# Layer 1's input features in another order, so that the recurrence's output is multiplied straight to its rows

## The chip, the cores and the metric

One core of a Trainium2 chip. The metric is the device time of the whole kernel in microseconds, as a median of runs. TensorE (PE) multiplies, VectorE (DVE) and ScalarE (ACT) do elementwise work and copies, GpSimd (POOL) a little of it, and SyncE (SP) issues nearly all transfers. TensorE writes to PSUM, eight banks of 128 partitions with 512 float32 each; everything else lies in SBUF.

## The reference

A gated recurrence (4 batches, 8 heads, 768 steps, 48 features a head) is followed by two layers of two matrices each. The recurrence's output y becomes x, one row per token with its 8 heads side by side (384 features). Layer 1 has a softplus between its matrices, layer 2 a piecewise square.

```python
def _attn_ref(q, k, v, f_logit):
    f = 1.0 / (1.0 + np.exp(-f_logit))
    state = np.zeros((B, H, D, D), dtype=np.float32)
    for t in range(S):
        state = f[:, :, t, :, None] * state + np.einsum('bhd,bhe->bhde', k[:, :, t], v[:, :, t])
        y[:, :, t] = np.einsum('bhd,bhde->bhe', q[:, :, t], state)

def _moe_ref(x, w_in, w_out):          # n_tokens, d_model, d_ff = 3072, 384, 2048
    h = x @ w_in
    g = np.maximum(h, 0.0) + np.log1p(np.exp(-np.abs(h)))
    return (g @ w_out).astype(np.float32)

x = np.ascontiguousarray(attn_out.transpose(0, 2, 1, 3)).reshape(B * S, H * D)
x = _moe_ref(x=x, **moe_kwargs)
return _moe2_ref(x=x, **moe2_kwargs)
```

## The kernel before

**Units.** The recurrence is worked in 24 units n, one of 128 steps of one batch (6 units a batch, c is the unit's place in its batch). Each unit handles the 8 heads as 4 pairs: a counts the pairs (NA = 4), hh is the head within a pair. A pair's two heads lie on partitions 0 to 47 and 64 to 111 (R = 112 rows in all). `load(n)` issues four transfers, for f, k, q and v, into three buffers of each in turn (`t_f`, `t_k`, `t_q`, `vz`); unit 3 borrows tiles of layer 1. `pre(n)` turns f into running products (`ip`, a scan on VectorE), scales k and q by them (L579) and transposes k (L608) into `ks`. `main(n)` multiplies k by q (L628) for both heads of each pair, masks the result into `am` (L636, or L643 and L644), multiplies `ks` by v for the new state (`dmm`, L656), and then forms y in one PSUM bank `py` (`ymm`): L671 adds V times `am`, L677 adds the old state `s1` times q where there is one (20 of the 24 units). `py` has 112 rows used, one pair's 128 steps beside the other (a x 128 columns). All these products are in float32, and the profile shows each as two records of TensorE. L685 and L688 update the state `sst`.

**From y to x.** Layer 1 reads x as 3 groups (m) of 128 features by tokens. The rows of `py` aren't the features' places, so y is copied to a staging tile `ys` on ScalarE and then moved by transfers from SBUF to SBUF, six for a unit: two that carry three pairs each, and four pieces of the fourth pair. The order of features which this gives (48 of each of six heads, then the fourth pair in pieces) is matched in the load of layer 1's first matrix, in two transfers for a chunk (`load_w`, L450 and L451). For units 0 to 3 (`whole`, the first block of 512 tokens) y stays float32 (L700) and the six moves go out on ScalarE's own queue (L717) to `xr2`. For the other units y is split into a high part (L702, ScalarE) and the rest (L703, VectorE), both go to `ys`, and eight moves a unit go out on SP's queue (L429, the helper `dma`) to `xhl`, a ring of 1024 tokens.

**The layers.** Each layer goes over 6 blocks of 512 tokens, and in a block over 16 chunks c of 128 hidden features. `hmm` (L747) forms a chunk's hidden features in one bank, `act1` or `act2` apply the function, `second` (L821 to L823, for the first block L826) adds the chunk's part of the output, two chunks later. In the first block the products are float32, 3 for a chunk and 3 behind it; in all others there are 9 and 9 with rounded operands. In the first block the weights of layer 1 also arrive: a chunk's two pieces are loaded into one of two `stg` buffers, converted by three passes on VectorE (L478, L481, L483) and written by a transfer to `w_l` (L487, shown as wl<-wa). In the second block each is split in two.

**The order.** Every operation is registered with its cost, what it reads and what it writes (`Order.add`). A planner (`Order.schedule`) simulates the engines with these costs and gives each engine's order of work, which is then fixed; TensorE's due times come from the order of registration. Where a copy can be done on either of two engines (`copy_any`, `inc_any`, `either`) the planner picks. Of the recurrence, units 0 to 3 are registered ahead of layer 1, the others between the steps of its blocks (`attn_upto`). Transfers on SP's queue go out in the planner's order, and one that waits for its data holds those behind it; the same holds on ScalarE, whose queue also carries its activations.

## Time and profile before

| | us |
|---|---|
| median of 3 runs | 949.88 |
| lowest, highest | 946.69, 950.42 |
| the profiled execution's own time | 949.62 |
| its span, first to last instruction | 947.8 |
| TensorE busy | 922.9 (97%) |
| VectorE busy | 655.7 (69%) |
| ScalarE busy | 640.3 (68%) |

All times of the trace are microseconds from the span's start. Busy time of an engine is the union of its records; TensorE's records overlap (they are pipelined), and its weight loads (PEld) run beside them. In a row of instructions, out<-in names tiles, the shapes are partitions x elements, x is a count, and a bracket at the end is the idle time of the engine just before and what ended it. SPq and ACTq are queues that issue transfers. PEclk is the granted clock of TensorE as a share of 2.4 GHz.

### The profile page before, as it was taken

The page shows a single profiled execution, that of the slowest core. Times are in us where ns is not written, and L with a number is a line of the kernel's source. Part 1 is how long each engine was busy: PE and PEld are TensorE (multiplying, and loading weights), DVE is VectorE, ACT ScalarE, POOL GpSimd, SP SyncE. Part 2 cuts the span into 40 slices and gives each one's busy share as a digit, 9 for nine tenths or more (in the row PEclk, how much of TensorE's full clock was granted, in tenths as well). Part 3 has the DMA queues.
Part 4 walks back from the last instruction along what each step waited for, and adds up shares of the span by engine and source line. Part 5 has one row for each costly group of instructions (what it writes and reads, how often), then busy time and mean ns, then how long its engine had stood idle before and what let it go on. Part 6 is the DMA issues. An engine that isn't in the chain of part 4 may idle for free.

```text
span 947.8 us, 13531 instructions
## 1 busy us (share of the span) xinstructions
PE 922.9 (97%) x4936; PEld 720.0 (76%) x4936; DVE 655.7 (69%) x1032; ACT 640.3 (68%) x1143; POOL 76.8 (8%) x91
## 2 busy tenths in 40 slices
PE   8599999999999999999999999999999999999997
PEld 7444457877787878877887888888888888888885
DVE  7789988986877768656899995454464464554542
ACT  4366668976967877766887868889874544544443
POOL 1002021001100010010003010010010010100000
PEclk9899999999999999999999999999999999999999
DMA  9678755344212331120152356766630100200001
GB/s 247 173 224 252 223 165 170 119 119 134 82 48 78 97 105 37 50 85 18 51 194 72 101 178 189 201 202 219 205 140 1 66 1 1 67 1 0 35 1 37
DMA packets 106890, 104.00 MB, mean 110 GB/s; under 512 B 8000, under 2 KB 89920, under 8 KB 106816
## 3 DMA queue, kind: packets, MB, share of 16 engines
q1 hardware_dynamic: 104896, 102.27, 35.8%
q10 hardware_dynamic: 1920, 0.79, 0.4%
q8 instruction: 41, 0.67, 0.3%
q14 instruction: 33, 0.27, 0.1%
HBM read 78.64 MB, written 9.44 MB: 93 GB/s over the span
## 4 chain that ended last, share of the span: by engine, by line
PE 88%; DMA 3%; DVE 3%; ACT 2%; SPq 1%; issue 1%; ACTq 0%; POOL 0%; DVEq 0%
PE bank L747 41%; PE bank L821 13%; PE bank L822 12%; PE bank L823 12%; PE bank L826 3%; PE bank L628 2%; PE bank L671 2%; PE bank L677 1%; SPq L429 1%; DMA t_k<-in_k_dram 1%; DMA stg<-in_moe_w_in_dram 1%; PE bank L656 1%; DMA xr<-ys 1%; DMA g<-in_k_dram 1%; DVE wa L481 1%
## 5 line engine op out<-in xcount | busy, mean ns | idle before, releaser
L747 PE MATMUL bank<-xhl,wh 128*128 128x512 f32 x840 | 260.6, 392 | 0.0
L747 PEld LDWEIGHTS bank<-xhl,wh 128*128 128x128 f32 x840 | 158.4, 189 | 32.4
L747 PE MATMUL bank<-xhl,wl 128*128 128x512 f32 x420 | 167.9, 400 | 3.4 <-DVE tl L784 3.4
L821 PE MATMUL bank<-gh,wl 128*128 128x512 f32 x420 | 164.3, 391 | 0.0
L823 PE MATMUL bank<-gl,wh 128*128 128x512 f32 x420 | 163.9, 390 | 0.0
L822 PE MATMUL bank<-gh,wh 128*128 128x512 f32 x420 | 163.6, 389 | 0.0
L424 ACT CAST gh<-tl 128x512 fp32r<-128x512 f32 x176 | 109.0, 619 | 78.3 <-DVE tl L807 49.5
L807 DVE TENSOR_TENSOR tl<-bank,te 128x512 f32<-128x512 f32 x96 | 66.3, 691 | 70.1 <-ACT te L806 70.1
L809 DVE TENSOR_TENSOR gl<-tl,gh 128x512 fp32r<-128x512 f32 x96 | 67.5, 703 | 60.8 <-ACT gh L424 60.7
L747 PEld LDWEIGHTS bank<-xhl,wl 128*128 128x128 f32 x420 | 79.1, 188 | 23.6 <-DVE tl L784 4.2
L777 ACT ACTIVATE te<-bank 128x512 f32<-128x512 f32 x96 | 57.0, 593 | 55.5 <-PE bank L747 55.2
L823 PEld LDWEIGHTS bank<-gl,wh 128*128 128x128 f32 x420 | 78.9, 188 | 17.4 <-DVE gl L792 1.0
L802 ACT ACTIVATE te<-bank 128x512 f32<-128x512 f32 x96 | 57.1, 594 | 51.4 <-PE bank L747 51.2
L821 PEld LDWEIGHTS bank<-gh,wl 128*128 128x128 f32 x420 | 78.9, 188 | 16.7 <-ACT gh L424 0.2
L822 PEld LDWEIGHTS bank<-gh,wh 128*128 128x128 f32 x420 | 78.9, 188 | 16.2
L806 ACT ACTIVATE te<-te 128x512 f32<-128x512 f32 x96 | 60.6, 631 | 41.5 <-DVE te L804 41.5
L782 DVE SCALAR_TENSOR_TENSOR te<-tu,te 128x512 f32<-128x512 f32 x96 | 67.0, 698 | 28.5 <-ACT tu L420 27.9
L804 DVE TENSOR_SCALAR te<-te 128x512 f32<-128x512 f32 x96 | 45.2, 471 | 52.6 <-ACT te L802 52.6
L792 DVE TENSOR_TENSOR gl<-tl,gh 128x512 fp32r<-128x512 f32 x80 | 55.3, 691 | 22.1 <-ACT gh L424 21.9
L784 DVE SCALAR_TENSOR_TENSOR tl<-bank,tl 128x512 f32<-128x512 f32 x96 | 65.8, 685 | 6.5 <-ACT tl L780 6.5
L747 PE MATMUL bank<-xhl,wxh 128*128 128x512 f32 x216 | 67.0, 391 | 0.0
L420 ACT ACTIVATE tu<-te 128x512 f32<-128x512 f32 x96 | 60.5, 630 | 2.1 <-DVE te L782 0.2
(110 smaller groups left out, 1394.7 us busy)
## 6 DMA issues: line engine op xcount, KB each, us to landing
stg<-in_moe_w_out_dram SPq DMA_DIRECT2D x64, 384.0 KB, 4.0
stg<-in_moe_w_in_dram SPq DMA_DIRECT2D x32, 384.0 KB, 3.8
stg<-in_moe_w_in_dram SPq DMA_DIRECT2D x32, 288.0 KB, 4.3
t_f<-in_f_logit_dram SPq DMA_DIRECT2D x23, 256.0 KB, 3.6
t_k<-in_k_dram SPq DMA_DIRECT2D x23, 256.0 KB, 4.0
t_q<-in_q_dram SPq DMA_DIRECT2D x23, 256.0 KB, 4.0
xhl<-ys SPq DMA_DIRECT2D x80, 72.0 KB, 2.3
wl<-wa SPq DMA_DIRECT2D x14, 384.0 KB, 3.0
```

Source lines behind the costliest of these rows:

```text
L420: "act": (c_act(n), lambda: nc.scalar.activation(out=o, in_=x, func=AF.Identity, bias=1.0))}
L424: "act": (c_act(n, ps), lambda: nc.scalar.copy(o(), x()))}
L747: nc.tensor.matmul(o, l, r, start=(j == 0), stop=(j == n - 1))
L782: do("dve", c_dve(N), lambda: nc.vector.scalar_tensor_tensor(out=e, in0=u, scalar=-1.0, in1=e, op0=ALU.add, op1=ALU.subtract), [ku, ke], [ke])
L784: do("dve", c_dve(N), lambda: nc.vector.scalar_tensor_tensor(out=l, in0=h, scalar=0.0, in1=l, op0=ALU.max, op1=ALU.add), [kb, kl], [kl])
L802: do("act", c_act(N, True), lambda: nc.scalar.activation(out=r, in_=h, func=AF.Relu, scale=0.5, bias=0.5), [kb], [kr])
L806: do("act", c_act(N), lambda: nc.scalar.activation(out=r, in_=r, func=AF.Square), [kr], [kr])
L807: do("dve", c_dve(N), lambda: nc.vector.tensor_tensor(out=l, in0=h, in1=r, op=ALU.max), [kb, kr], [kl])
L809: do("dve", c_dve(N), lambda: nc.vector.tensor_tensor(out=gl, in0=l, in1=gh.bitcast(F32), op=ALU.subtract), [kl, kgh], [kgl])
L821: nc.tensor.matmul(o, ol, gh, start=(c == 0), stop=False)
L822: nc.tensor.matmul(o, oh, gh, start=False, stop=False)
L823: nc.tensor.matmul(o, oh, gl, start=False, stop=(c == NFC - 1))
```

## The change

The order of x's 384 features becomes: the first 32 features of all 8 heads (256), then the last 16 of all 8 heads (128). So each of the three groups of 128 features is made of four strips of 32 rows, and y is multiplied strip by strip. The host pads v to 64 values a head: 32 features, then 16 more and 16 zeros for the first head of a pair, or 16 zeros and then 16 features for the second; and it puts the rows of layer 1's first matrix in the same order. `ymm` has 16 products with `am`, each of 32 columns of V into a strip of 32 rows of `py` (groups m = 0 and 1 by head; group 2 by pair, both heads added into one strip), and, with a state, 4 products over all 112 rows for group 2 and 8 over 48 rows for groups 0 and 1. The copy from PSUM (ScalarE, or either engine for the first block) and the subtraction (VectorE) write layer 1's input `xr2`, or `xh` and `xl`, directly, 384 columns in place of 512. `ys` and all its moves are gone. The state's tiles and the state product are 64 columns wide in place of 48, v's loads 64 values a head, and layer 1's first matrix is loaded in one transfer a chunk. The general path, which isn't run on this data, is changed to the same order (left out here). The costs that the planner is told for `dmm` and `ymm` stay as they were.

```diff
@@ -324,7 +326,7 @@
     NFC = FF // P
     NK = DM // P
     R = 112
-    E2 = 2 * D
+    V2 = P
     XR = 1024
     WN = NK * P + DM
     wide = w_in1.dtype != F32
@@ -386,7 +388,7 @@
     mask = attp.tile([P, P], F32, name="mask")
     cap = attp.tile([P, NA, P], F32, name="cap")
     ident = attp.tile([P, P], F32, name="ident")
-    vz = buf("vz", [P, NA * E2], NQ, pool=attp)
+    vz = buf("vz", [P, NA * V2], NQ, pool=attp)
 
     t_f = buf("t_f", [P, NA, P], 3, pool=attp)
     t_k = buf("t_k", [P, NA, P], NQ, pool=attp)
@@ -394,10 +396,8 @@
     ip = buf("ip", [P, NA, P], 2, pool=attp)
     ks = buf("ks", [P, NA, R], 2, pool=attp)
     am = buf("am", [P, NA, P], 2, pool=attp)
-    sst = buf("sst", [P, NA, D], 2, pool=attp)
-    t2 = attp.tile([P, NA, D], F32, name="t2")
-
-    ys = buf("ys", [P, 2, NA, P], 2, pool=attp)
+    sst = buf("sst", [P, NA, 64], 2, pool=attp)
+    t2 = attp.tile([P, NA, 64], F32, name="t2")
 
     warm = attp.tile([P, P], F32, name="warm")
     nc.vector.memset(warm, 0.0)
@@ -446,11 +446,7 @@
         else:
             si = st[:, 0:NK * P].rearrange("p (m f) -> p m f", m=NK)
             so = st[:, NK * P:WN]
-        if layer == 1:
-            dma(si[0:96], cols[0:288, :].rearrange("(m p) f -> p m f", p=96), [], [("stg", s, 0)], 295e3)
-            dma(si[96:128], cols[288:384, :].rearrange("(m p) f -> p m f", p=32), [], [("stg", s, 1)], 98e3)
-        else:
-            dma(si, cols.rearrange("(m p) f -> p m f", p=P), [], [("stg", s, 0), ("stg", s, 1)])
+        dma(si, cols.rearrange("(m p) f -> p m f", p=P), [], [("stg", s, 0), ("stg", s, 1)])
         dma(so, rows, [], [("stg", s, 2)])
         return s
 
@@ -551,18 +547,19 @@
 
         if n == 3:
             g = [x.rearrange("p (a t) -> p a t", a=NA) for x in g_0]
-            return (g[2], g[0], g[1], t_u[0][:, 0:NA * E2]), (("gh", 2), ("gh", 0), ("gh", 1), ("tu", 0))
+            return (g[2], g[0], g[1], t_u[0][:, 0:NA * V2]), (("gh", 2), ("gh", 0), ("gh", 1), ("tu", 0))
         i = n if n < 3 else (n - 1) % NQ
         return (t_f[i], t_k[i], t_q[i], vz[i]), (("t_f", i), ("t_k", i), ("t_q", i), ("vz", i))
 
     def load(n):
+
 
 
         b, c = divmod(n, NCH)
         t = slice(c * P, c * P + P)
         tiles, keys = inputs_of(n)
         for o, i, key, size in zip(tiles, (f_logit[b, :, :, t], k[b, :, :, t], q[b, :, :, t], v[b, t]), keys,
-                                   (262e3, 262e3, 262e3, 197e3)):
+                                   (262e3, 262e3, 262e3, 262e3)):
             dma(o, i, [], [key], size)
         attn_keys.update(keys)
 
@@ -653,8 +650,8 @@
                 for a in range(NA):
                     for hh in range(2):
                         r = slice(64 * hh, min(64 * hh + 64, R))
-                        nc.tensor.matmul(pd[r, a * D:(a + 1) * D], ks[z][:, a, r],
-                                         V[:, (2 * a + hh) * D:(2 * a + hh + 1) * D], start=True, stop=True)
+                        e = (2 * a + hh) * 64
+                        nc.tensor.matmul(pd[r, a * 64:(a + 1) * 64], ks[z][:, a, r], V[:, e:e + 64], start=True, stop=True)
 
             ado("pe", 500, dmm, [("ks", z)] + kv, [kd])
         yield
@@ -663,67 +660,49 @@
         k1, k2 = ("sst", c % 2), ("sst", (c + 1) % 2)
 
         def ymm():
-            for a in range(NA):
-                for hh in range(2):
-
-                    m = 64 if hh == 0 else D
-                    e = (2 * a + hh) * D
-                    nc.tensor.matmul(py[64 * hh:64 * hh + m, a * P:(a + 1) * P], V[:, e:e + m], am[hh][:, a, :],
-                                     start=(c == 0 or a == 0), stop=(c == 0))
+
+
+            for h in range(H):
+                m, g = divmod(h, 4)
+                nc.tensor.matmul(py[32 * g:32 * g + 32, m * P:(m + 1) * P], V[:, 64 * h:64 * h + 32],
+                                 am[h % 2][:, h // 2, :], start=(m == 0), stop=False)
+            for hh in range(2):
+                for a in range(NA):
+                    e = (2 * a + hh) * 64 + 32
+                    nc.tensor.matmul(py[32 * a:32 * a + 32, 2 * P:3 * P], V[:, e:e + 32], am[hh][:, a, :],
+                                     start=False, stop=(c == 0 and hh == 1))
             if c > 0:
                 for a in range(NA):
-                    for hh in range(2):
-                        r = slice(64 * hh, 64 * hh + D)
-                        nc.tensor.matmul(py[r, a * P:(a + 1) * P], s1[r, a, :], Q[r, a, :],
-                                         start=False, stop=(a == NA - 1))
+                    nc.tensor.matmul(py[32 * a:32 * a + 32, 2 * P:3 * P], s1[0:R, a, 32:64], Q[0:R, a, :],
+                                     start=False, stop=False)
+                for h in range(H):
+                    m, g = divmod(h, 4)
+                    r = slice(64 * (h % 2), 64 * (h % 2) + D)
+                    nc.tensor.matmul(py[32 * g:32 * g + 32, m * P:(m + 1) * P], s1[r, h // 2, 0:32], Q[r, h // 2, :],
+                                     start=False, stop=(m == 1))
 
         ado("pe", (2000 if c else 1070), ymm, kv + [("am", 0), ("am", 1), kq] + ([k1] if c else []), [ky])
         if c < NCH - 1:
-            pdv = pd[0:R, 0:NA * D].rearrange("p (a e) -> p a e", a=NA)
+            pdv = pd[0:R, 0:NA * 64].rearrange("p (a e) -> p a e", a=NA)
             new, old = pdv, [kd]
             if c > 0:
-                ado("dve", c_dve(NA * D), lambda: nc.vector.tensor_tensor(
+                ado("dve", c_dve(NA * 64), lambda: nc.vector.tensor_tensor(
                     out=t2[0:R], in0=pdv, in1=s1[0:R], op=ALU.add), [kd, k1], [("t2",)])
                 new, old = t2[0:R], [("t2",)]
-            ado("dve", c_dve(NA * D), lambda: nc.vector.tensor_tensor(
-                out=s2[0:R], in0=new, in1=pcall[0:R, n, :][:, :, None].broadcast_to([R, NA, D]), op=ALU.mult),
+            ado("dve", c_dve(NA * 64), lambda: nc.vector.tensor_tensor(
+                out=s2[0:R], in0=new, in1=pcall[0:R, n, :][:, :, None].broadcast_to([R, NA, 64]), op=ALU.mult),
                 old + [("pcall", n)], [k2])
         yield
         xo = (n * P) % XR
         sl = slice(xo, xo + P)
-        pyv = py[0:R].rearrange("p (a t) -> p a t", a=NA)
-        xs = xo // P
-        whole = n * P < BLOCKS1[0]
-        Y = ys[z]
-        kyh, kyl = ("ys", z, 0), ("ys", z, 1)
-        if whole:
-            ado("act", c_act(NB, True), lambda: nc.scalar.copy(Y[0:R, 0], pyv), [ky], [kyh])
+        pyv = py[:, 0:NK * P].rearrange("p (m t) -> p m t", m=NK)
+        kx, kxh, kxl = ([(x, xo // P, u) for u in range(6)] for x in ("x0", "xh", "xl"))
+        if n * P < BLOCKS1[0]:
+            ado(copy_any(NK * P, lambda: xr2[:, :, sl], lambda: pyv, True), 0, None, [ky], kx)
         else:
-            ado("act", c_act(NB, True), lambda: nc.scalar.copy(Y[0:R, 0].bitcast(F32R), pyv), [ky], [kyh])
-            ado("dve", c_dve(NB), lambda: nc.vector.tensor_tensor(
-                out=Y[0:R, 1].bitcast(F32R), in0=pyv, in1=Y[0:R, 0], op=ALU.subtract), [ky, kyh], [kyl])
-
-        moves = [(0, 48, 0, None, 0), (64, 112, 48, None, 1),
-                 (0, 32, 96, 0, 2), (32, 48, 96, 1, 3), (64, 80, 112, 1, 4), (80, 112, 96, 2, 5)]
-        for lo, up, to, m, u in moves:
-            src = slice(lo, up)
-            dst = slice(to, to + up - lo)
-            size = (up - lo) * P * 4 * (3 if m is None else 1)
-            if whole:
-                if m is None:
-                    o, i = xr2[dst, 0:3, sl], Y[src, 0, 0:3, :]
-                else:
-                    o, i = xr2[dst, m, sl], Y[src, 0, 3, :]
-                do("act", 500, lambda o=o, i=i: nc.scalar.dma_start(out=o, in_=i), [kyh], [("x0", xs, u)],
-                   delay=1700 + size / 250)
-            else:
-                if m is None:
-                    for j in range(2):
-                        dma(xhl.bitcast(F32)[dst, j, 0:3, sl], Y[src, j, 0:3, :], [(kyh, kyl)[j]],
-                            [(("xh", "xl")[j], xs, u)], size)
-                else:
-                    dma(xhl.bitcast(F32)[dst, :, m, sl], Y[src, :, 3, :], [kyh, kyl],
-                        [("xh", xs, u), ("xl", xs, u)], 2 * size)
+            ado("act", c_act(NK * P, True), lambda: nc.scalar.copy(xh[:, :, sl], pyv), [ky], kxh)
+            ado("dve", c_dve(NK * P), lambda: nc.vector.tensor_tensor(
+                out=xl[:, :, sl], in0=pyv, in1=xh[:, :, sl].bitcast(F32), op=ALU.subtract), [ky] + kxh, kxl)
         ndone[0] = n + 1
         yield
 
@@ -1033,7 +1012,15 @@
         x[:, :, 0:D] = inputs[name].reshape(B, NA, 2, S, D).transpose(0, 2, 4, 1, 3)
         inputs[name] = x.reshape(B, P, NA, S)
 
-    inputs["v"] = inputs["v"].transpose(0, 2, 1, 3).reshape(B, S, H * D)
+
+    x, v = inputs["v"].transpose(0, 2, 1, 3), _np.zeros((B, S, H, 64), _np.float32)
+    v[:, :, :, 0:32] = x[:, :, :, 0:32]
+    v[:, :, 0::2, 32:48] = x[:, :, 0::2, 32:48]
+    v[:, :, 1::2, 48:64] = x[:, :, 1::2, 32:48]
+    inputs["v"] = v.reshape(B, S, H * 64)
+
+    w = inputs["moe_w_in"].reshape(H, D, -1)
+    inputs["moe_w_in"] = _np.concatenate([w[:, 0:32].reshape(32 * H, -1), w[:, 32:D].reshape(16 * H, -1)])
 
     nc = _bacc.Bacc("TRN2", target_bir_lowering=False, num_devices=1, dynamic_dma_scratch_size=2048)
     arrays, args = {}, []
```

## Rows read from the trace of the kernel before

**Rows 1.** The page, part 1: busy us (share of the span) xinstructions
```profile
PE 922.9 (97%) x4936; PEld 720.0 (76%) x4936; DVE 655.7 (69%) x1032; ACT 640.3 (68%) x1143; POOL 76.8 (8%) x91
```

**Rows 2.** Stages: us, busy (x) of PE PEld DVE ACT POOL, PEclk, DMA, GB/s
```profile
34.50:45.30 10.80, 2.17 (x36) 1.57 (x32) 5.75 (x13) 3.72 (x7) 0.20 (x1) 0.72 0.72 189
45.30:54.40 9.10, 8.56 (x28) 3.96 (x28) 5.92 (x11) 5.07 (x9) 0.00 (x0) 0.77 0.53 158
54.40:145.00 90.60, 90.12 (x378) 43.68 (x379) 86.49 (x129) 59.72 (x101) 13.25 (x12) 1.00 0.74 216
```

**Rows 3.** Timeline of TensorE, 24 to 46 us: start, us, instruction, count, idle
```profile
34.32 1.08 PE L677 MATMUL bank<-g,sst 48*48 48x128 f32 x16
...
45.32 1.22 PE L747 MATMUL bank<-xr,wl 128*128 128x512 f32 x1 [7.38 <-DMA xr<-ys]
```

**Rows 4.** Chain of waits, 24 to 62 us: start, us, what
```profile
45.34 4.88 PE bank L747 x6
...
59.83 2.58 PE bank L747 x6
```

**Rows 5.** Timeline of ScalarE and its queue, 16 to 46 us
```profile
32.81 4.97 ACTq L717 DMA_DIRECT2D xr<-ys  x6
...
39.02 0.57 ACT L700 COPY ys<-bank 112x512 f32<-112x512 f32 x1
...
39.62 4.15 ACTq L717 DMA_DIRECT2D xr<-ys  x6
```

**Rows 6.** Timeline of VectorE, 20 to 55 us
```profile
24.45 0.69 DVE L579 TENSOR_TENSOR ip<-ip,g 128x512 f32<-128x512 f32 x1 [2.03 <-ACT g L594]
```

**Rows 7.** Transfers of the whole span: out<-in, count, size, median us to landing
```profile
xhl<-ys SPq DMA_DIRECT2D x80, 72.0 KB, 2.3
wl<-wa SPq DMA_DIRECT2D x14, 384.0 KB, 3.0
...
vz<-in_v_dram SPq DMA_DIRECT2D x23, 192.0 KB, 2.7
...
xhl<-ys SPq DMA_DIRECT2D x40, 32.0 KB, 1.9
```

**Rows 8.** Groups by line and shape: busy us, mean ns of one, idle before
```profile
L703 DVE TENSOR_TENSOR ys<-bank,ys 112x512 fp32r<-112x512 f32 x20 | 13.7, 686 | 3.1 <-ACT ys L702 3.0
...
L685 DVE TENSOR_TENSOR t<-bank,sst 112x192 f32<-112x192 f32 x16 | 5.6, 349 | 1.0 <-PE bank L656 1.0
```

**Rows 9.** Timeline of TensorE, a unit's y, 440 to 448 us
```profile
446.25 1.09 PE L671 MATMUL bank<-am,vz 128*64 128x128 f32 x16
447.27 1.08 PE L677 MATMUL bank<-t_q,sst 48*48 48x128 f32 x16
```

**Rows 10.** Groups by shape, TensorE, 446.20 to 446.26 us (V's part begins)
```profile
L671 PE MATMUL bank<-am,vz 128*64 128x128 f32 x1 | 0.3, 324 | 0.0
L671 PE MATMUL bank<-am,vz 128*48 128x128 f32 x1 | 0.3, 310 | 0.0
```

**Rows 11.** Groups by shape, TensorE, 425.53 to 425.72 us (a state product begins)
```profile
L656 PE MATMUL bank<-vz,ks 128*48 128x48 f32 x4 | 0.4, 217 | 0.0
L656 PE MATMUL bank<-vz,ks 128*64 128x48 f32 x3 | 0.4, 234 | 0.0
```

**Rows 12.** Timeline of SP's queue, 196 to 245 us
```profile
224.71 5.25 SPq L429 DMA_DIRECT2D xhl<-ys  x8
...
230.70 0.60 SPq L429 DMA_DIRECT2D t_k<-in_k_dram  x1
```

**Rows 13.** Timeline of VectorE, 224 to 246 us
```profile
236.42 0.69 DVE L579 TENSOR_TENSOR t_k<-t_k,ip 128x512 f32<-128x512 f32 x1 [4.33 <-DMA t_k<-in_k_dram]
```

**Rows 14.** Timeline of TensorE, 237 to 241 us
```profile
240.10 0.50 PE L747 MATMUL bank<-xhl,wl 128*128 128x512 f32 x1 [1.98 <-DVE tl L784]
```

**Rows 15.** Chain of waits, 230 to 254 us
```profile
240.10 3.79 PE bank L747 x9
...
247.36 2.04 PE bank L747 x9
```

More of the change, by code (lines that the diff above doesn't have):

```diff
@@ L205, in general_path @@
                     for b in range(B):
-                        nc.sync.dma_start(
-                            out=vb[rows, b * NA:(b + 1) * NA, :],
-                            in_=v[b, bass.ds(t, 1), :].rearrange("o (a h e) -> o a h e", a=NA, h=2)[:, :, hh, :].broadcast_to([D, NA, D]))
+                        vt = v[b, bass.ds(t, 1), :].rearrange("o (a h e) -> o a h e", a=NA, h=2)[:, :, hh, :]
+                        for e, to in ((slice(0, 32), slice(0, 32)), (slice(32 + 16 * hh, 48 + 16 * hh), slice(32, D))):
+                            nc.sync.dma_start(out=vb[rows, b * NA:(b + 1) * NA, to],
+                                              in_=vt[:, :, e].broadcast_to([D, NA, to.stop - to.start]))
                 nc.scalar.activation(out=f, in_=f, func=AF.Exp, scale=-1.0)
@@ L220, in general_path @@
                 for b in range(B):
-                    nc.sync.dma_start(
-                        out=xN[bass.ds(t + b * S, 1), :].rearrange("o (a h e) -> h (o a) e", a=NA, h=2),
-                        in_=ys[:, b * NA:(b + 1) * NA, :])
+                    for e, to in ((slice(0, 32), slice(0, 32 * H)), (slice(32, D), slice(32 * H, DM))):
+                        nc.sync.dma_start(
+                            out=xN[bass.ds(t + b * S, 1), to].rearrange("o (a h e) -> h (o a) e", a=NA, h=2),
+                            in_=ys[:, b * NA:(b + 1) * NA, e])
         for layer, wi, wo in ((1, w_in1, w_out1), (2, w_in2, w_out2)):
```

## The prediction

> **What bounds the kernel now.** I read the page first: TensorE is busy 922.9 of 947.8 us, 97% [rows 1]. So a change pays only where it takes work off TensorE, or takes away one of the few stretches in which TensorE stands still. The table of stages shows where these lie [rows 2]: from 34.5 to 45.3 us TensorE works 2.17 us; in the next 9.1 us it is busy, but at a granted clock of 0.77, a mean over its two levels of 1.2 and 2.4 GHz; from 54.4 to 145 us it is busy 90.12 of 90.60 us. VectorE is busy 86.49 us of that last stage, which matters below.
>
> The chain of waits and TensorE's own rows name the reason. The first product of layer 1 starts at 45.32 us after 7.38 us of waiting for a transfer xr<-ys [rows 3], and the six matmuls from there take 4.88 us, where six of the same size take 2.58 us at full clock [rows 4]. The queue of ScalarE shows what lies ahead: the six moves of one unit hold its issue for 4.97 us, those of the next for 4.15 us, and between them the copy of unit 3 out of PSUM begins at 39.02 us [rows 5], though that unit's last product was done at 34.32 + 1.08 = 35.40 us [rows 3]. VectorE, too, stood 2.03 us at 24.45 us for an activation that lay behind moves [rows 6]. The run's own time is 949.62 us, 1.8 us more than the span and 0.26 us under the median of three (949.88); the sum is made against 949.62.
>
> **Part 1, the moves ahead of layer 1.** 24 transfers on ScalarE's queue go (units 0 to 3, six each); the copy writes layer 1's input itself. From unit 3's end at 35.40 us I take 2.0 us off, the wait of VectorE that the moves caused [rows 6], since VectorE paces these units. I add 0.6 us for the copy (0.57 us for 512 columns [rows 5], now 384, and a hop), and 0.5 us because v comes in rows of 64 values: its 192 KB a unit [rows 7] become 256 KB, four units of 64 KB more at some 200 GB/s [rows 2], 1.3 us, of which I count less than half, since weights and the later units' inputs are in the same stream. Layer 1 begins at 34.5 us in place of 45.3: -10.8 us. Bounds: 33 us, if unit 3 gains more than that one wait, and 37 us, if it gains nothing and the longer loads count in full. Without the long stop the clock has no cause to fall: six matmuls at 2.58 in place of 4.88 us, -2.3 us [rows 4].
>
> What is late next is the weights of the third chunk. Before, two chunks, one product of a unit and a short wait filled the 9.1 us to the third [rows 2], and VectorE had had until then to convert it. Now it is wanted 12 us earlier, behind a conversion on VectorE and a write wl<-wa that alone takes 3.0 us to land [rows 7]: +1.0 us, bounds 0 and 3.
>
> Then VectorE: from 34.5 to 145 us it had 5.75 + 5.92 + 86.49 = 98.2 us of work [rows 2], and there were 110.5 us for it; with the 11 to 12 us gone there are 98 to 99. Its work hardly changes: the subtraction shrinks from 512 to 384 columns, the operations on the state grow from 192 to 256 columns, some 0.15 us less and 0.13 us more a unit (by the two durations of [rows 8], 1.05 ns a column). If VectorE could be no fuller than the 95% of the stage before, it would need 102.8 us, 4 us given back; at 100% nothing is given back. I take +3.0 us; as bounds 0 and the whole of part 1 (a rival below).
>
> **Part 2, y in four columns.** For a unit with state the old code issues 8 products of V and 8 of the state, two records each, 16 and 16 [rows 9]. The two heads of a pair go to two column groups of the array, and these run side by side: within 60 ns one record of 64 columns and one of 48 have begun [rows 10], although in the program's order the second record of the 64 stands before the first of the 48. So 16 records take eight steps: from the first start to the last is 1.09 less one record of 0.27 us, 0.82 us in seven gaps, 0.117 us a step [rows 9]. The new code issues 16 products of V, of 32 columns each, and 12 of the state. Over four column groups V's 32 records are again eight steps; the state's are two (four products over 112 rows) and four (eight products over 48 rows), six where there were eight. If four groups run side by side as two do, that is 2 x 0.117 us in each of the 20 units with state, -4.7 us; the four units without state keep eight steps. The other bound is two records at a time: then the 24 records more in a unit, at half a step of 0.0585 us, cost 1.4 us in each of 20 units, 28.1 us, and 16 more in each of four units 3.7 us, together +31.8 us. No row shows four groups at once. The nearest is the small product of V and ks: its two groups keep separate counts, four starts of the narrow one against three of the wide one, seven starts within 0.19 us, 27 ns apiece [rows 11]; four groups need four starts in 0.117 us, 29 ns apiece. So neither order nor the rate of issue speaks against four, and I take -4.7 us.
>
> The Trainium skill does speak against it: "TensorE: Matmul & The Clock Gate", Part 3, The mechanism, says that matmuls keep strict program order in both their starts and their ends. By that rule the two records of one product, both for one group, would go one behind the other before the next group's begin, and four groups would do no better than two: the +31.8 us. The trace disagrees with it for two groups, by [rows 10, 11]; no run here has four.
>
> The product of ks and V streams 64 columns in place of 48; its wide group's weights keep their width, and I count nothing for it, with 0.1 us a unit as the other bound, 2 us.
>
> **Part 3, the moves of units 4 to 23.** 160 transfers xhl<-ys leave SP's queue (80 of 72 KB, the others smaller) [rows 7], eight a unit, 5.25 us of issue for one unit [rows 12]. The copy on ScalarE and the subtraction on VectorE write the same columns, and are shorter; they must now wait for the matmuls that read those columns before, but the ring holds two blocks, and the block in question is done by then: nothing. What stands behind the moves on SP is the loads of q, k, v and f. At 224.71 us the moves hold SP, and t_k is issued at 230.70 us only [rows 12]; VectorE then waits 4.33 us for it [rows 13], TensorE 1.98 us for VectorE [rows 14], and its clock falls, so that nine matmuls take 3.79 in place of 2.04 us [rows 15]. That is 3.7 us with one cause. I take -3.0 us: bounds 0, if the loads wait for their buffers and not for SP, and -3.7. Layer 1's weights come in one transfer in place of two: SP issues fewer, off the path, nothing.
>
> Sum: 949.6 - 10.8 - 2.3 + 1.0 + 3.0 - 4.7 - 3.0 = 932.8, so 933 us.
>
> **The rivals.** First, two at a time: the four column groups do the work of two, because a product's two records hold the array's order or the streams share one path. All else stays: 932.8 + 4.7 + 31.8 = 969 us, slower. What the moves give is 12 us with part 3, so it decides from a pace at which a unit's y costs 0.6 us more than now, under half of the way to that bound. For it: no row has four. Against it: [rows 10, 11]. Chance 0.12.
>
> Second, VectorE is the bound until 145 us: it is nearly full there already, and the earlier start only makes TensorE wait for it later. Then part 1 is worth nothing: 949.6 - 4.7 - 3.0 = 942 us. For it: 86.49 of 90.60 us [rows 2]. Against it: TensorE stood still for 0.5 us in all of that stage. Chance 0.15.
>
> Third, nothing much: the planner, whose list of work is another now, makes new stops such as that of 236 us, SP's loads were held by their buffers all along, and part 1 comes short too: 945 to 952 us. Chance 0.05.
>
> **How the numbers follow.** The forecast has 0.68, with a range of its own of 927 to 942 us: the good bounds of part 1 (-1.5, -1.0, -3.0) and part 3 (-0.7) below, 2.5 of the start, 4 of VectorE and weights and 3 of SP above. Faster by over 0.5% (below 944.9 us; about what a measurement of this kernel can tell from no change) are the forecast and most of the second rival, 0.81. Within 0.5%: the rest of it and the third, 0.07. Slower: the first rival, 0.12. The range of 925 to 946 us takes in forecast and second rival, and leaves out the first and most of the third.
>
> **What would show it.** The first product of layer 1 at 33 to 37 us at full clock, and no stop of TensorE over 2 us from there to 145 us; V's part of a unit 1.1 us long with 32 records, the state's 0.9 us with 24, against 2.0 and 1.5 us if two run at a time; VectorE over 95% busy in the first block; no wait for t_k near 230 us. It would be wrong if V's records start in pairs, if the first block's end moves by less than its start, or if new stops appear behind 145 us.

## The result and the profile after

The changed kernel takes 934.47 us (median of four runs, 932.67 to 937.27) where the kernel before takes 950.15 us beside it (946.69 to 951.89): a ratio of 0.984, with a 95% interval of 0.9805 to 0.9879. Its profiled run took 934.49 us with a span of 932.8 us, 15.0 us less than the span before. The forecast was 933 us.

In the kernel after, the products of layer 1 are in L726 (first half) and L805 or L800 to L802 (second half), V's products of y in L667 and L672, the state's in L676 and L681, and the product of ks and V in L654. The page's first part, as in [rows 1] (busy us, share of the span, instructions): 544 matmul records more, and 7.3 us less of TensorE.

```profile
PE 915.6 (98%) x5480; PEld 711.9 (76%) x5480; DVE 656.5 (70%) x1030; ACT 638.0 (68%) x1145; POOL 71.9 (8%) x91
```

TensorE's timeline of after, from unit 2's y to layer 1 (start, us, instruction, count, idle before it), as in [rows 3, 9]:

```profile
25.15 0.65 PE L667 MATMUL bank<-am,vz 128*32 128x128 f32 x16
25.61 0.62 PE L672 MATMUL bank<-am,vz 128*32 128x128 f32 x16
26.04 0.40 PE L676 MATMUL bank<-t_q,sst 112*32 112x128 f32 x8
26.38 0.64 PE L681 MATMUL bank<-t_q,sst 48*32 48x128 f32 x16
26.95 1.26 PE L625 MATMUL bank<-g,g 48*128 48x128 f32 x16
...
31.29 0.64 PE L681 MATMUL bank<-g,sst 48*32 48x128 f32 x16
32.53 2.84 PE L726 MATMUL bank<-xr,wl 128*128 128x512 f32 x6 [0.60 <-ACT xr L424]
```

Three things are to be seen. Unit 3's last product ends at 31.93 us, where it ended at 35.40 us. Layer 1 begins at 32.53 us in place of 45.32, after 0.60 us of waiting for ScalarE's copy and for no transfer, and its six products run at full clock at once. And a unit's y is 56 records in 1.80 us, from 25.15 to 26.95, where 32 records took 2.02 us before: from 446.25 us [rows 9] to the start of layer 1's next product.

```profile
448.27 0.50 PE L747 MATMUL bank<-xhl,wl 128*128 128x512 f32 x1
```

That four column groups are at work at once shows in the groups by shape of 428.90 to 428.93 us, where V's part of a late unit begins, against [rows 10]:

```profile
L667 PE MATMUL bank<-am,vz 128*32 128x128 f32 x4 | 0.3, 297 | 0.0
```

Four records have begun within 30 ns. V's 32 records then take 0.89 us from their first start to that of the state's (25.15 to 26.04), eight steps of 0.11 us. Before, V's eight steps took 1.02 us (446.25 to 447.27) and the state's 1.00, and now the state's six take 0.91, so the 0.22 us do not lie where the forecast had them. They are two steps all the same: some 0.1 us more goes by at one place in both kernels, before between V's part and the state's, now between the state's two kinds (0.34 us from 26.04 to 26.38 for two steps, which take 0.23 inside one kind, in the kernel with two more steps below).

The stages show where time is given back (columns as in [rows 2]). First two of before, from its first product of layer 1 to its second block, and its last block of layer 1:

```profile
45.32:148.41 103.09, 102.08 (x444) 49.97 (x444) 95.23 (x142) 67.90 (x115) 13.25 (x12) 0.98 0.71 206
476.97:543.86 66.89, 66.06 (x290) 53.68 (x288) 66.82 (x99) 55.02 (x95) 8.01 (x3) 1.00 0.35 118
```

Of after, the stretch ahead of layer 1, the first block, the block in which before stopped for t_k, and the last block of layer 1:

```profile
20.00:32.50 12.50, 11.93 (x256) 9.91 (x248) 12.50 (x27) 3.13 (x6) 0.20 (x1) 1.00 0.61 185
...
32.53:133.35 100.82, 96.83 (x513) 46.52 (x513) 99.36 (x152) 70.50 (x120) 11.19 (x13) 1.00 0.74 239
...
216.11:297.57 81.46, 81.46 (x641) 65.14 (x639) 63.48 (x100) 63.84 (x117) 7.95 (x12) 1.00 0.23 71
...
459.49:528.49 69.00, 66.88 (x289) 53.51 (x288) 68.39 (x100) 55.26 (x95) 4.82 (x3) 1.00 0.35 115
```

VectorE had waits ahead of layer 1 before [rows 6]; now it works 12.50 of 12.50 us there. In the first block it is busy 99.36 of 100.82 us (95.23 of 103.09 before), and TensorE stands still for 3.99 us where it stood for 1.01. The waits of the block say for whom (us in total, times, longest): most of it in the second half of layer 1 for VectorE's g, the rest for ScalarE's copy of ks and, 0.3 us, for GpSimd. Before, all of the 1.01 us were waits for VectorE.

```profile
PE bank L805 <- DVE g L766: 2.9, 3, 1.8
PE bank L654 <- ACT ks L424: 0.7, 1, 0.7
```

From 216 to 298 us TensorE never stands still: the stop of [rows 12 to 15] is gone. SP's queue in that stretch holds yT and the loads alone, and t_k goes out in its turn:

```profile
221.81 2.83 SPq L429 DMA_DIRECT2D yT<-xr  x3
225.61 0.55 SPq L429 DMA_DIRECT2D t_k<-in_k_dram  x1
```

The last block of layer 1 became longer: 69.00 us for 66.89. It has three stops, of 1.32, 0.39 and 0.42 us, the last at 493.82 us, where before had one of 0.82 us (504.48 us). TensorE's timeline of after has the longest:

```profile
488.11 0.50 PE L802 MATMUL bank<-gl,wh 128*128 128x512 f32 x1 [1.32 <-DVE gl L771]
```

VectorE's timeline just before them, and GpSimd's, which forms sums for layer 2's first block there:

```profile
483.37 0.69 DVE L769 TENSOR_TENSOR tl<-tl,te 128x512 f32<-128x512 f32 x1
483.98 2.39 DVE L840 TENSOR_TENSOR xhl<-xr,xhl 128x512 fp32r<-128x512 f32 x2
486.29 1.77 DVE L771 TENSOR_TENSOR gl<-tl,gh 128x512 fp32r<-128x512 f32 x1
487.98 1.77 DVE L761 SCALAR_TENSOR_TENSOR te<-tu,te 128x512 f32<-128x512 f32 x1
```

```profile
483.61 1.60 POOL L842 TENSOR_TENSOR acc<-acc,xhl 128x512 f32<-128x512 f32 x1 [52.16 <-DVE xhl L840]
485.91 3.30 POOL L842 TENSOR_TENSOR acc<-acc,xhl 128x512 f32<-128x512 f32 x2 [0.69 <-DVE xhl L840]
```

Beside the three sums, three operations of VectorE that take 0.69 us elsewhere take some 1.8 us (one of them is in the row of 2.39). This cause the prediction does not have at all.

### The profile page after: what moved, and what is told of

It reads as the page before. It is cut to its first block, busy times and chain, and to the rows that moved or that the text cites. A ratio compares the mean times of both kernels' runs of the same rounds, so it can differ in the third digit from the quotient of the medians.

```text
span 932.8 us, 14237 instructions
## 1 busy us (share of the span) xinstructions
PE 915.6 (98%) x5480; PEld 711.9 (76%) x5480; DVE 656.5 (70%) x1030; ACT 638.0 (68%) x1145; POOL 71.9 (8%) x91
## 4 chain that ended last, share of the span: by engine, by line
PE 88%; DVE 6%; DMA 2%; issue 1%; ACT 1%; POOL 0%; SPq 0%; DVEq 0%; ACTq 0%
PE bank L726 40%; PE bank L800 12%; PE bank L801 12%; PE bank L802 12%; PE bank L805 3%; PE bank L625 3%; PE bank L667 1%; PE bank L681 1%; PE bank L654 1%; PE bank L672 1%; DVE gl L771 1%; DVE tl L763 1%; DMA xr<-yT 1%; DVE te L761 1%; PE bank L605 1%
## 5 line engine op out<-in xcount | busy, mean ns | idle before, releaser
L726 PE MATMUL bank<-xhl,wh 128*128 128x512 f32 x840 | 259.5, 390 | 0.0
L726 PEld LDWEIGHTS bank<-xhl,wh 128*128 128x128 f32 x840 | 157.7, 188 | 32.2 <-issue 0.2
L726 PE MATMUL bank<-xhl,wl 128*128 128x512 f32 x420 | 168.4, 401 | 0.4 <-DVE tl L763 0.4
L802 PE MATMUL bank<-gl,wh 128*128 128x512 f32 x420 | 163.7, 390 | 1.7 <-DVE gl L771 1.7
L800 PE MATMUL bank<-gh,wl 128*128 128x512 f32 x420 | 164.2, 391 | 0.0
L788 DVE TENSOR_TENSOR gl<-tl,gh 128x512 fp32r<-128x512 f32 x96 | 69.7, 727 | 61.8 <-ACT gh L424 60.2
L726 PEld LDWEIGHTS bank<-xhl,wl 128*128 128x128 f32 x420 | 78.8, 188 | 22.0 <-DVE tl L763 2.9
L802 PEld LDWEIGHTS bank<-gl,wh 128*128 128x128 f32 x420 | 78.8, 188 | 19.2 <-DVE gl L771 2.6
L800 PEld LDWEIGHTS bank<-gh,wl 128*128 128x128 f32 x420 | 78.8, 188 | 17.2 <-ACT gh L424 0.3
L771 DVE TENSOR_TENSOR gl<-tl,gh 128x512 fp32r<-128x512 f32 x80 | 56.6, 708 | 22.3 <-ACT gh L424 21.6
L726 PE MATMUL bank<-xhl,wxh 128*128 128x512 f32 x216 | 66.9, 391 | 0.0
```

Of the source, the lines that this page charges most:

```text
L726: nc.tensor.matmul(o, l, r, start=(j == 0), stop=(j == n - 1))
L771: do("dve", c_dve(N), lambda: nc.vector.tensor_tensor(out=gl, in0=l, in1=gh.bitcast(F32), op=ALU.subtract), [kl, kgh], [kgl])
L788: do("dve", c_dve(N), lambda: nc.vector.tensor_tensor(out=gl, in0=l, in1=gh.bitcast(F32), op=ALU.subtract), [kl, kgh], [kgl])
L800: nc.tensor.matmul(o, ol, gh, start=(c == 0), stop=False)
L802: nc.tensor.matmul(o, oh, gl, start=False, stop=(c == NFC - 1))
```

## The experiments

Each kernel below is the changed kernel with one edit, so "against after" is against its 934.47 us; run once more beside the last ones it gave 934.35 us (933.78 to 935.08). Line numbers of the variants are their own.

**The moves of units 0 to 3 come back.** What do 24 moves ahead of layer 1 cost, with y in four columns all the same?

```diff
-            ado(copy_any(NK * P, lambda: xr2[:, :, sl], lambda: pyv, True), 0, None, [ky], kx)
+            ado("act", c_act(NK * P, True), lambda: nc.scalar.copy(Y[:, 0], pyv), [ky], [("ys", z, 0)])
+            for u, (lo, up, m) in enumerate(MOVES):
...
+                do("act", 500, lambda lo=lo, up=up, ms=ms: nc.scalar.dma_start(
+                    out=xr2[lo:up, ms, sl], in_=Y[lo:up, 0, ms, :]), [("ys", z, 0)], [("x0", xo // P, u)],
```

> The changed kernel, but units 0 to 3 go again through a staging tile and six moves a unit on ScalarE's queue, of the sizes that the kernel before had. If the moves ahead of layer 1 are what held its start: the first product of layer 1 back at about 44 us in place of 32.5, the granted clock low behind it, and VectorE's slack in the first block back, so 934.5 + 12.8 + 2.3 - 3.5 = about 946 us. If VectorE gives back all of an earlier start in any case: no more than 937 us, with a first block that is shorter by what the start is later.

Measured: 943.92 us (942.02 to 945.47), 0.9921 of before (0.9895 to 0.9947), 9.5 us over after. TensorE's timeline:

```profile
43.58 1.12 PE L657 MATMUL bank<-vz,ks 128*64 128x64 f32 x16 [4.89 <-ACT ks L427]
45.69 7.95 PE L736 MATMUL bank<-xr,wl 128*128 128x512 f32 x12 [0.99 <-DMA xr<-ys]
```

Layer 1 begins at 45.69 us, behind a transfer xr<-ys again, 13.2 us later than in after; of these the profiled span keeps 10.8 us (943.6 against 932.8). The median lies some 2 us under the 946 us that I expected. So the moves ahead of layer 1 held its start, and VectorE gives back only a part: the second rival, for which the start would be worth nothing, falls.

**The moves of units 4 to 23 come back**, eight a unit on SP's queue.

```diff
+            ado("act", c_act(NK * P, True), lambda: nc.scalar.copy(Y[:, 0].bitcast(F32R), pyv), [ky], [kyh])
...
+                    for j in range(2):
+                        dma(xhl.bitcast(F32)[lo:up, j, :, sl], Y[lo:up, j], [(kyh, kyl)[j]], [(("xh", "xl")[j], xo // P, u)], size)
```

> The changed kernel, but units 4 to 23 go again through a staging tile and eight moves a unit on SP's queue. If SP's hold made the loads of k late: a wait of VectorE for t_k of 3 us or more in the blocks behind the first, TensorE waiting for VectorE, about 938 us. If the loads wait for their buffers in any case, or that stop was chance of the planner's order: within 1 us of 934.5.

Measured: 942.91 us (941.79 to 943.97), 0.9917 of before (0.9887 to 0.9947), 8.4 us over after by the medians and 7.3 by the spans. The sign was right and the size was not. There is no stop at 236 to 244 us; TensorE's timeline has others:

```profile
144.20 0.50 PE L739 MATMUL bank<-xhl,wl 128*128 128x512 f32 x1 [1.80 <-DVE tl L776]
...
229.98 0.50 PE L739 MATMUL bank<-xhl,wl 128*128 128x512 f32 x1 [1.39 <-DVE tl L776]
```

What lies ahead of the second shows in the timelines of SP's queue and of ScalarE:

```profile
215.19 5.25 SPq L432 DMA_DIRECT2D xhl<-ys  x8
...
221.88 0.59 SPq L432 DMA_DIRECT2D t_f<-in_f_logit_dram  x1
```

```profile
227.04 0.63 ACT L581 ACTIVATE t_f<-t_f 128x512 f32<-128x512 f32 x1 [1.35 <-DMA t_f<-in_f_logit_dram]
```

Eight moves hold SP for 5.25 us, t_f goes out behind them, ScalarE waits for it with an operation of layer 1 behind, VectorE waits 1.15 us for that one, and TensorE for VectorE. The stop at 144.20 us has the same links: eight moves of 5.47 us from 130.20 us, t_f behind them at 135.76, and ScalarE waiting 2.40 us for it at 139.11. This is the chain of the prediction with another load and one more engine in it. Behind the start of layer 1 TensorE waits 10.8 us in this kernel (889.26 of 900.06 us busy) and 6.1 in after (887.15 of 893.26), 4.7 of the 7.3 us.

The start of the last block of layer 1 is 5.7 us later than in after, and 1.4 us more come in the stretch of GpSimd's sums, when every unit is done. So moves on SP cost more than the one stop that I had priced, and the stop falls elsewhere.

**All moves come back**: both edits together, which leaves of the change the four columns and the wider tiles.

> Both sets of moves back, so that of the change only the four columns, the wider state and the loads of v and of layer 1's matrix are left. If the parts add up: 934.5 + 11.6 + 3.7 = about 950 us less what they share, 947 to 950. If four columns bring what I read from a unit's y (0.22 us in each of 20 units) and nothing else hangs on them, it is 4 us below the kernel before, about 946 us.

Measured: 955.50 us (ten runs, 952.81 to 958.55), 1.0047 of before (1.0027 to 1.0067): missed, 5 us slower than before instead of faster. One of its stops is the stop of [rows 12 to 15] once more; the timelines of SP's queue, of VectorE and of TensorE:

```profile
226.52 6.44 SPq L432 DMA_DIRECT2D xhl<-ys  x8
...
233.68 0.60 SPq L432 DMA_DIRECT2D t_k<-in_k_dram  x1
```

```profile
238.77 0.69 DVE L579 TENSOR_TENSOR t_k<-t_k,ip 128x512 f32<-128x512 f32 x1 [3.55 <-DMA t_k<-in_k_dram]
```

```profile
242.46 0.69 PE L746 MATMUL bank<-xhl,wl 128*128 128x512 f32 x1 [1.94 <-DVE tl L783]
```

Eight moves hold SP for 6.44 us, t_k goes out behind them, VectorE waits 3.55 us and TensorE 1.94 us for VectorE: the chain of the prediction, link by link. Against before, this kernel loses 3.7 us between the start of the second and of the third block of layer 1, and 4.1 us in layer 1's last and layer 2's first block, when no unit is left; the four columns should have gained 4.4. In those two blocks stand GpSimd's sums (below), and TensorE's idle time there, 3.06 us against 0.82 before, covers about half of the 4.1. The rest I cannot place. Over all that stands behind the start of layer 1 TensorE waits 11.5 us in this kernel (891.88 of 903.38 us busy) and 4.4 in before (891.50 of 895.86), so most of the excess is waiting.

**All moves, and a planner that knows the new prices**: is the excess just an order planned with wrong durations? The same edit was also made to the changed kernel.

```diff
-            ado("pe", 500, dmm, [("ks", z)] + kv, [kd])
+            ado("pe", 610, dmm, [("ks", z)] + kv, [kd])
...
-        ado("pe", (2000 if c else 1070), ymm, kv + [("am", 0), ("am", 1), kq] + ([k1] if c else []), [ky])
+        ado("pe", (1800 if c else 1070), ymm, kv + [("am", 0), ("am", 1), kq] + ([k1] if c else []), [ky])
```

> All moves back as in the run before that had both sets (955.5 us), with the same true costs for the planner. If that kernel lay 9 us above my sum (946 us) because of stops that its particular order made: some of them go, 946 to 951 us. If the wider loads, the wider state or the moves themselves make them: 954 to 957 us.

> The changed kernel, but the planner is told what the profile shows for the recurrence's products: 1800 ns in place of 2000 for a unit's y with state, 610 in place of 500 for the state product. Nothing else is changed; the engines' orders come out otherwise. If the time hangs on the parts and hardly on the planner's order: within 1.5 us of 934.5. If order alone moves it as far as the stops of single runs suggest: 2 to 5 us to either side.

Measured: 956.99 us with the moves (955.40 to 960.18), 1.0068 of before (1.0042 to 1.0094), and 932.93 without (932.64 to 934.68), 0.9827 (0.9804 to 0.9850). This other order moves either by some 1.5 us; the excess of the moves stays, with stops at other places. Its cause stays open.

**Two more steps of the state.** Four products more in each unit with state, into columns that nothing reads: if a product of all four groups is two steps, this is 20 x 0.23 us.

```diff
+                for a in range(NA):
+                    nc.tensor.matmul(py[32 * a:32 * a + 32, 3 * P:4 * P], s1[0:R, a, 32:64], Q[0:R, a, :],
+                                     start=False, stop=False)
```

> The changed kernel with four products more in each of the 20 units with state, in the same four column groups, into columns of the PSUM bank that nobody reads: two steps of a column group more, as the state's part had before (eight and not six); the planner is told nothing of it. If a step of all four groups costs 0.11 us of TensorE's time and TensorE sets the end: 0.22 us in each of the units behind the start of layer 1, 17 of them, 3.7 us, up to 4.4 with the other three: 938 to 939 us. If the recurrence's products hide behind other waits: within 1 us of 934.5.

Measured: 938.86 us (937.68 to 939.77), 0.9881 of before (0.9858 to 0.9904), 4.4 us over after, 4.6 by the spans: 0.22 to 0.23 us a unit. TensorE's timeline has the eight records more (L679) between the old ones:

```profile
26.09 0.40 PE L676 MATMUL bank<-t_q,sst 112*32 112x128 f32 x8
26.32 0.40 PE L679 MATMUL bank<-t_q,sst 112*32 112x128 f32 x8
26.65 0.64 PE L684 MATMUL bank<-t_q,sst 48*32 48x128 f32 x16
```

Eight records of four groups cost 0.23 us, two steps. The price of part 2 holds, and what leaves TensorE there leaves the end.

**V column by column.** The same 16 products of V, but all of one column group ahead of the next group's. If the groups were wholly independent, their order would cost nothing; if there were one queue, it would cost all.

```diff
-            for h in range(H):
-                m, g = divmod(h, 4)
+            for g in range(4):
+                for h in (g, g + 4):
+                    m = h // 4
```

> The changed kernel, but V's 16 products in a unit are issued column group by column group (all four of the first, then all of the second, and so on) and not turn by turn; the planner's order is the same. If each group takes its records from one queue in program order, whatever the others do: 32 records one behind the other at 0.11 us, 3.5 us for V's part in place of 0.9, 2.6 us more in each of 24 units, some 50 to 60 us in all, 985 to 995 us. If the groups are independent and the queue reaches past 8 records and their loads: V's part stays at 0.9 to 1.2 us, 934 to 940 us.

Measured: 965.45 us (964.29 to 966.24), 1.0164 of before (1.0140 to 1.0188), 31 us over after: neither of the two. TensorE's timeline of one unit:

```profile
441.87 0.62 PE L668 MATMUL bank<-am,vz 128*32 128x128 f32 x4
442.33 0.27 PE L672 MATMUL bank<-am,vz 128*32 128x128 f32 x1
442.34 0.30 PE L668 MATMUL bank<-am,vz 128*32 128x128 f32 x1
...
444.48 0.64 PE L681 MATMUL bank<-t_q,sst 48*32 48x128 f32 x16
445.05 0.50 PE L726 MATMUL bank<-xhl,wl 128*128 128x512 f32 x1
```

The first four records of a group run alone, 0.11 us apart; the next group's first record begins beside the fifth. So it goes from group to group: 8 + 4 + 4 + 4 = 20 steps, 2.2 us, and y takes 3.18 us in place of 1.80. Groups do run side by side, but here a record waits until the group ahead of it in the program has four left. That a queue reaches only so far would make this; the run doesn't show the cause. The time is near the first rival's (969 us), by way of the program's order.

**VectorE relieved in the first block.** The third pass of converting layer 1's weights on VectorE goes (it supplies the three lowest bits of each mantissa).

```diff
+            if layer == 2:
-            do("dve", c_dve(n), lambda o=o, lo=lo: nc.vector.scalar_tensor_tensor(
+                do("dve", c_dve(n), lambda o=o, lo=lo: nc.vector.scalar_tensor_tensor(
```

> The changed kernel, but the third of the three passes that convert layer 1's weights (the three lowest bits of the mantissa) is left out: 16 operations of VectorE of 1.0 us less ahead of 134 us. If VectorE, full in layer 1's first block, is what gives back 3.5 us of the earlier start: the stops of TensorE from 41 to 134 us (3.3 us of idle time) go, 931 to 932 us. If the weights' transfers or the planner's order make those stops: within 1 us of 934.5.

Measured: 931.52 us (930.00 to 932.88), 0.9800 of before (0.9777 to 0.9823), 3.0 us under after by the medians and 1.7 by the spans (931.1 against 932.8); the interval overlaps that of after. The first product comes later, at 35.30 us, and yet the second block begins at the same time, 133.48 us; the stage from 43 us on in this run:

```profile
43.00:134.00 91.00, 90.73 (x483) 43.64 (x484) 82.52 (x122) 63.58 (x108) 12.31 (x12) 1.00 0.75 240
```

With VectorE at 82.52 of 91.00 us, TensorE stands still for 0.27 us, and for 1.22 us in the whole block, where after has 3.99. So with less work on VectorE the stops go, as expected. But the block ends no earlier than in after (133.35 us): it began 2.8 us later, and such a start leaves VectorE more time in any case. The run thus fits VectorE as the cause, and after's waits name it, but it doesn't show it alone; and the gain of the profiled run lies behind the first block.

**GpSimd's sums.** First a try at moving them: the sums of layer 2's first block are handed to the planner later in its list.

```diff
+        if bi:
+            add()
+        else:
+            adds.append(add)
```

> The changed kernel, but the three sums on GpSimd over the first block of layer 2's input (L842) are registered in layer 2's first block and not in layer 1's last. If GpSimd's sums are what made VectorE's operations on SBUF tiles take 1.7 us in place of 0.7 at 484 to 490 us, and these the stops of TensorE there: the stops are gone, layer 1's last block is 2 us shorter, 932.5 us. If VectorE is late there by its own load of work (weights of layer 2, three splits): within 0.5 us of 934.5.

Measured: 933.21 us (932.98 to 933.37), 0.9810 of before (0.9781 to 0.9840). The planner put the sums as early as before (482.86 us), so the run decides nothing; it shows the stop once more, at another place: VectorE has an operation of 1.79 us at 487.62 us, and TensorE waits 1.67 us for VectorE at 492.51 us.

Then the 18 sums go to VectorE itself, alone and with the planner's new prices.

```diff
-        do("pool", c_ptt(TB), lambda: nc.gpsimd.tensor_tensor(
+        do("dve", c_dve(TB), lambda: nc.vector.tensor_tensor(
             out=acc[0], in0=acc[0], in1=XL.bitcast(F32), op=ALU.add), wl_ + [("w2x",), ("acc",)], [("acc",)])
```

> The changed kernel, but the 18 sums over layer 2's input (L842) run on VectorE in place of GpSimd. If GpSimd's sums are what made VectorE's operations on SBUF tiles take 1.7 us there: none of these takes over 1.1 us near 484 to 490 us, the stops of TensorE of 1.5 and 0.6 us there are gone, 932 to 933 us, though VectorE has 18 operations of 0.7 us more. If VectorE's own load is the cause: longer, 935 to 936 us.

> The changed kernel with the sums on VectorE and the true costs. If both help or the costs do nothing: 931 to 933 us. If the new order makes stops of its own: 934 to 937 us.

Measured: 932.89 us (932.69 to 934.65) and 933.24 us (932.38 to 933.63), 0.9826 (0.9803 to 0.9849) and 0.9821 (0.9799 to 0.9842) of before. VectorE's timeline in the first of them:

```profile
488.17 0.68 DVE L842 TENSOR_TENSOR acc<-acc,xhl 128x512 f32<-128x512 f32 x1
```

VectorE does a sum in 0.68 us, less than it lost to one of GpSimd's, no operation is stretched there, and the stops of 488 to 494 us are gone, so the sums made them; a new one of 0.85 us stands at 532.25 us, for ScalarE. What they cost the kernel is not settled: the gain, 1.6 us or 0.2%, is as large as the stops, but within what these runs can tell apart; the two intervals overlap that of after, and the kernels of 932.93 and 933.21 us came as low with the sums on GpSimd.

## Why the prediction held, step by step

The terms, each as measured in the profiled runs; a minus is time saved.

| step | predicted, us | measured, us | from |
|---|---|---|---|
| start of layer 1 | -10.8 | -12.8 | 45.32 to 32.53 |
| clock at the start | -2.3 | -2.3 | six products at full clock at once |
| weights, VectorE in the first block | +1.0, +3.0 | 0, +3.0 | TensorE's idle time, 1.01 to 3.99 |
| four columns | -4.7 | -4.4 | 20 x 0.22; 0.7 of it lies ahead of the start |
| t_k's stop | -3.0 | -3.7 | its whole price before; no idle time, 216 to 298 |
| sums beside VectorE | none | +2.1 | 66.89 to 69.00 |

With the 0.7 counted once the measured terms make 17.4 us less; TensorE's last product moved by 15.4 us (941.18 to 925.79). Of the 2 us between the two some 0.9 are the product of ks and V: 10.86 us in 256 records stand behind the start of layer 1, for 9.98 in 240 before. The rest, small losses, I have not placed. The forecast's 933 us is thus right by its main terms, and close by the luck that a stop which I did not foresee, these losses and a better start nearly cancel.

**The start** was under-sized. I took 2.0 us off unit 3's end, one wait of VectorE [rows 6]; it came 3.5 us earlier (35.40 to 31.93), of which three units' 0.22 us are the four columns. VectorE paces these units, and without the moves it is busy 12.50 of 12.50 us. The bounds, 33 and 37 us, just missed the 32.53. The longer loads of v cost nothing that shows.

**What is late next** was VectorE, as forecast: 99% busy in the first block. The third chunk's weights were not late; no wait for them shows. Of the 3.0 us of waits more than before 1.9 are for VectorE (2.9 for 1.0), 0.7 for ScalarE's copy of ks and 0.3 for GpSimd, and the kernel without the third pass agrees without showing it alone. Of 1.0 and 3.0 us that I had put down 3.0 came, a third of it from engines that I had not named.

**Four columns.** The step of 0.117 us was worked out from two groups and held for four (0.11 us); the two kernels that add steps and reorder them confirm both the price and the pace. By the Trainium skill, "TensorE: Matmul & The Clock Gate", Part 3, The mechanism, the matmuls would have kept strict order in their starts and ends, and by the prediction's working part 2 would have been +31.8 us. The trace of after disagrees where the products change group at every step, and the kernel with V column by column shows where something like that rule returns: 965.45 us. The rule was a fair rival; this kernel's order of products is what decided it. I counted nothing for the wider product of ks and V; it is a small part of the 0.9 us above, which also hold one more unit's product behind the start. Where a product of layer 1 follows, that one starts 0.61 us after the first of the 16 records (408.40 to 409.01), before 0.59 (425.54 to 426.13).

**The moves on SP's queue** gave their stop back, but with the moves alone put back the time rises by 7 to 8 us and not by 3.7, and with all of them by 21. The step that failed is "one cause": I priced the one stop that the trace of before had and took it for the price of the moves. That the moves make SP late, and that this reaches TensorE, the stops at 144, 230 and 242 us of the two kernels show; at which place it happens differs from kernel to kernel. Why the moves and the four columns together are slower than before stays open.

**Not foreseen**: the sums on GpSimd. The change does not touch them; it only shifted what stands beside them. The trace of before had the row to learn it from, GpSimd's three sums at 496.80 us in 8.16 us, and beside them operations of VectorE of 1.06, 1.79 and 1.17 us (501.05, 502.04 and 504.35 us) that take 0.55, 0.69 and 0.69 elsewhere, behind the 8% of the page. The first and the third rival fell by the time, the second by the first experiment.

## What to carry to other kernels

When column groups of the array are to work at once, change the group with every product in the program's order: the same products sorted by group cost 31 us here, 1.4 us a unit. Small moves cost most in the queue that issues them, and ahead of the first product that waits for them; price every transfer that stands behind them, not only the stop that the trace happens to show. When an early stage is shortened, look first which engine is nearly full in the next one, and which operations of a lightly used engine will now fall beside it.

## What the runs showed of the hardware

GpSimd's sum and VectorE can hold each other up, and it depends on the operands. Beside a sum VectorE's operations on two SBUF tiles took up to 1.80 us in place of 0.69, and the longest of before's 18 sums took 4.89 us, the shortest 1.31. One that reads a bank of PSUM beside a sum did not change; GpSimd's row and VectorE's from after:

```profile
555.40 1.35 POOL L842 TENSOR_TENSOR acc<-acc,xhl 128x512 f32<-128x512 f32 x1 [0.69 <-DVE xhl L840]
```

```profile
556.29 0.69 DVE L786 TENSOR_TENSOR tl<-bank,te 128x512 f32<-128x512 f32 x1 [0.70 <-ACT te L785]
```

One that reads a single SBUF tile was stretched too, beside two sums from 616.45 us; elsewhere it takes 0.42 us:

```profile
618.57 1.52 DVE L783 TENSOR_SCALAR te<-te 128x512 f32<-128x512 f32 x1
```

The end of the stretched ones fits a wait for the sum: the one that starts at 486.29 us ends at 488.06, some 0.5 us after the first of two sums of 1.65 us from 485.91. The Trainium skill, "SBUF — State Buffer", section Who interferes with whom, states an exclusive lock between a VectorE instruction with two SBUF inputs and a GpSimd instruction that reads SBUF, and none where at most one input is in SBUF, as long as VectorE isn't in a mode that takes both ports. The trace agrees on the first with 1.77 us, and on the second with the 0.69 us of the operation that reads PSUM; by that rule the 1.52 us of the last row would need such a mode, and no run here shows which mode an operation is in.

The other is how far column groups of TensorE run ahead of the program's order: in the unit of the kernel with V column by column, the next group's first record begins beside the fifth of a group of eight, not earlier, so that four groups in sorted order take 20 steps and in alternating order eight.
